# A new order of tasks, engine choices and PSUM banks in a fused scan-and-MLP kernel on one core

## The chip, the cores and the metric

The kernel runs on one core of a Trainium2 chip. The core has five engines with instruction streams of their own: TensorE (PE, matrix multiplies; PEld is its weight load), VectorE (DVE), ScalarE (ACT), GpSimd (POOL) and SyncE (SP), which here only starts DMA transfers. The metric is the device time of one execution in microseconds (us); lower is better.

## The reference, cut to what matters

All tensors are bf16; L = 2048 rows, D = 448, F = 1792.

```python
x  = A_x                                   # (1, 2048, 448)
xn = layernorm(x)
# s: a complex diagonal recurrence over the 2048 rows
Lam_bar = exp(dt * Lam);  B_bar = ((Lam_bar - 1) / Lam)[:, None] * B
Bu  = xn @ B_bar.T                         # complex, 448 states
h_t = Lam_bar * h_{t-1} + Bu_t
s   = 2 * real(h @ C.T) + xn * Dskip
# g: an MLP on a second layernorm of the same rows
y = layernorm(xn)
g = silu(gelu(y @ w1 + b1) @ w2 + b2)
out = x + s * g
```

## The kernel before

**Groups.** The 2048 rows are worked in four groups of 512 (g = 0 to 3). A group has four tiles of 128 rows, named by block b and half r. `x_all` holds x, `xn_sb` and `xn2_sb` the first and second norm, `xnT` and `xn2T` their transposes (two buffers each, used by g mod 2).

**What a group does.** VectorE takes the statistics (`ln_stats`, L430 and L434), VectorE or GpSimd turns them into scale and shift (`ln_scale`, L477 to L487), VectorE (L497) or ScalarE (L498) applies them (`ln_apply`), and a DMA transposes the result (`xt`, L507; the queue's rows show it as L106). TensorE then computes
- `mm1(g, j)`, j = 0 to 6: `xn2T` times w1 into two PSUM banks (L648), 14 matmuls of 64 rows that run in pairs; ScalarE takes them out with gelu into `gT` (L729; in group 0 some are done in halves, L741);
- `bu(g, i)`, i = 0 to 3: `xnT` times B (`BT`, and for i = 3 its copy `BT3`; L648 and L668), taken out into `u_sb` by ScalarE (L665, L670) or VectorE (L666, L671);
- `mm2(g, b)`: `gT` times w2 (L762, after a bias matmul L754), taken out by ScalarE with silu into `g_sb` (L766);
- `ym(g, b, r)`: h times C plus xn times Dskip (L780, L783), multiplied with `g_sb` by VectorE (L786); x is added (L799, L790) and the rows go out by DMA.

The recurrence itself is `ssm(g)`, on VectorE: u is turned by the table `WT` (L684 to L688), seven scans run over 512 columns each (L692), ScalarE casts the result to `s_b` (L696; L697 or, on VectorE, L698), VectorE turns it back (L712 to L716) into `h_sb`. GpSimd carries the end state to the next group (L705 to L708). The tables `WT` and the matrices `CQ` (from C) and `DG` (from Dskip, L584 on GpSimd or L585 on VectorE) are made once, in `tables`, `cq` and `parameters`.

**What sets the order.** The program records some 500 tasks; each names the tiles that it reads and writes. Three lists at the top of the file then decide everything else. `ORDER` is the one sequence in which all tasks are handed to their engines, so it is the order of every engine's stream and of the DMA queue. `SECOND` names the tasks that take the second of two engines. `BANKS` gives each PSUM tile its bank; a tile waits until the earlier tile of its bank has been read. Each engine works its stream strictly in order and waits on semaphores for what it reads:

```python
        for k in SECOND:
            (plain[k] if isinstance(k, int) else self.named[k]).choose(1)
        order = [plain[k] if isinstance(k, int) else self.named[k] for k in ORDER]
        ...
        self.place(order)
        ...
        for t in order:
            ...
            for sem, val in need.items():
                if seen.get(sem, 0) < val:
                    eng.wait_ge(self.sems[sem], val)
                    seen[sem] = val
```

**The place of the first `bu`.** `bu(0, 3)` (L668) is the first multiply by B. It needs both `xnT` transposes of group 0 and `BT3`, which VectorE copies out of `BT` (L626) and partly clears (L627); the other `bu` need all four transposed parts of B (two of the real, two of the imaginary half). All of these come through SP's one queue, between the loads of w2 and those of C, together with the broadcast of Dskip to 128 partitions (`Dbc`), the load of x for group 3 (`x_all`) and the transposes of the next group (`xn2T`).

Of the kernel before, what the change touches and what calls it, by code (L numbers as in the profile page):

```python
# [203 lines left out]


ORDER = [int(k) if k.isdigit() else k for k in """
18 17 16 4 11 12 13 14 2 3 ST I0 I4 0 10 1 I1 I2 I6 74 75 76 19 20 79 80 81 77 84 82 85 7 15 89 90 T0 78 I5 86 21 T2 I3 87 9 91 94 92 83 I7
H000 PV T1 39 6 41 8 40 88 T3 42 93 117 38 22 23 H010 95 44 H020 99 H011 103 96 H021 100 101 24 25 26 35 37 224 222 226 34 144 228 31 H04 32
104 102 105 223 118 5 54 55 H05 109 45 43 33 123 47 106 122 H001 227 115 225 229 46 111 48 110 112 124 314 49 230 97 H06 98 H03 113 193 107
56 121 125 198 DH 28 202 30 50 53 52 63 116 60 126 127 129 114 108 131 128 132 134 58 59 61 64 65 120 199 200 119 27 203 318 312 316 234 235  # L210
206 204 207 311 315 241 237 205 231 57 62 67 69 130 232 36 313 317 29 70 194 208 195 209 196 135 238 136 145 166 197 236 137 233 U00 167 66
68 U02 160 U01 164 319 324 402 400 404 401 133 162 142 161 201 141 H13 H15 320 165 323 239 163 171 240 282 H11 H14 286 283 139 168 138 287
403 170 407 284 285 406 278 H12 172 169 H10 140 279 242 H16 146 72 325 276 178 180 173 U12 147 405 177 408 148 321 288 277 247 176 149 U11
280 289 143 248 174 179 150 322 175 U10 281 181 245 H20 152 151 153 243 246 183 184 244 182 156 154 290 365 295 293 410 294 297 249 188 189
73 155 190 413 186 326 296 185 291 157 191 158 330 250 366 329 159 192 71 210 218 254 253 255 211 327 51 187 258 219 216 212 412 217 H25 298
H22 261 263 375 292 H23 260 220 369 371 376 409 372 370 252 331 251 328 U20 338 262 332 259 221 U22 333 H26 H24 377 213 256 257 339 373 265
411 214 414 378 U21 341 416 336 337 264 H35 334 H36 266 267 268 462 464 374 H31 269 335 271 272 270 H21 273 274 275 465 418 342 454 455 343
344 419 367 299 305 307 420 301 463 368 300 348 352 H32 340 H30 306 415 456 349 H34 452 457 453 347 345 H33 460 461 417 458 U31 U32 351 308
346 423 350 302 309 459 424 U30 425 354 353 379 421 426 358 355 356 422 310 357 359 382 360 427 361 362 363 364 432 431 433 440 437 428 441
429 436 383 384 466 385 388 380 394 439 438 381 215 303 443 471 386 467 387 472 396 473 430 434 435 442 447 444 445 446 469 448 449 450 390  # L220
451 395 477 475 304 389 391 392 393 397 398 481 485 489 470 474 478 399 468 476 479 480 482 483 484 486 487 488 490 I9 I8 491 492
""".split()]
SECOND = [int(k) if k.isdigit() else k for k in """
70 72 78 83 88 115 116 146 152 163 183 187 231 234 235 240 241 270 319 323 324 326 327 329 330 339 359 415 416 418 419 424
""".split()]
BANKS = [int(k) if k.isdigit() else k for k in """
4 4 4 3 4 1 2 5 2 0 1 2 4 0 4 6 6 2 0 4 6 2 2 4 0 4 0 2 0 6 7 4 5 6 1 0 5 2 4 0 3 4 0 6 6 2 4 2 4 5 6 7 4 3 5 2 2 0 4 0 0 0 6 4 2 2 6 7 6 0
1 4 2 0 7 2 6 4 5 6 2 0 0 4 6 4 3 6 2 5 0 1 7 2 4
""".split()]


# [650 lines left out]
```

## Time and profile before

| what | value |
|---|---|
| median of 3 runs | 147.53 us (147.47 to 148.44) |
| the profiled execution | 148.12 us |
| its span, first to last instruction | 146.1 us, so 2.0 us lie around it |
| busy in the span | PE 141.0, DVE 128.3, ACT 103.6, POOL 42.5 us |
| granted TensorE clock | 1.00 |

A row of the timeline gives the start in us from the span's beginning, the time from there to the end of its last instruction, engine, line, operation, output and input, a count, and in brackets the idle time ahead of it with what ended it. Neighbouring instructions of an engine overlap a little, so the distance of two starts is what one costs the engine. In the chain of work the second number is the share of the path, without overlap. Rows of the queue with SPq give the time from issue to issue; a separate view gives the time from issue to landing.

### The profile page before, as it was taken

The page shows a single profiled execution, that of the slowest core. Times are in us where ns is not written, and L with a number is a line of the kernel's source. Part 1 is how long each engine was busy: PE and PEld are TensorE (multiplying, and loading weights), DVE is VectorE, ACT ScalarE, POOL GpSimd, SP SyncE. Part 2 cuts the span into 40 slices and gives each one's busy share as a digit, 9 for nine tenths or more (in the row PEclk, how much of TensorE's full clock was granted, in tenths as well). Part 3 has the DMA queues.
Part 4 walks back from the last instruction along what each step waited for, and adds up shares of the span by engine and source line. Part 5 has one row for each costly group of instructions (what it writes and reads, how often), then busy time and mean ns, then how long its engine had stood idle before and what let it go on. Part 6 is the DMA issues. An engine that isn't in the chain of part 4 may idle for free.

```text
span 146.1 us, 2863 instructions
## 1 busy us (share of the span) xinstructions
PE 141.0 (97%) x1092; PEld 72.7 (50%) x1092; DVE 128.3 (88%) x182; ACT 103.6 (71%) x148; POOL 42.5 (29%) x88
## 2 busy tenths in 40 slices
PE   6899999979999999999999999999999999999993
PEld 1477645524554435545553454554445455555563
DVE  2942994867899999989999998999999999999994
ACT  3349999959799989999989999916996510190300
POOL 2589498710000799650000006000009400000000
PEclk9999999999999999999999999999999999999999
DMA  4999989899796300000445400044003300003033
GB/s 104 268 318 361 327 176 132 70 279 151 138 108 139 72 4 17 19 0 18 82 80 139 90 18 25 0 81 80 4 0 99 99 0 7 0 0 99 0 126 126
DMA packets 32083, 14.08 MB, mean 96 GB/s; under 512 B 24131, under 2 KB 31686, under 8 KB 32070
## 3 DMA queue, kind: packets, MB, share of 16 engines
q1 hardware_dynamic: 31376, 13.83, 43.2%
q8 instruction: 8, 0.13, 0.4%
q10 hardware_dynamic: 694, 0.07, 0.4%
q14 instruction: 5, 0.04, 0.1%
HBM read 5.63 MB, written 1.84 MB: 51 GB/s over the span
## 4 chain that ended last, share of the span: by engine, by line
PE 91%; DVE 5%; DMA 1%; issue 1%; POOL 0%; DVEq 0%
PE psum L648 42%; PE psum L762 29%; PE psum L780 14%; PE psum L668 3%; PE psum L783 2%; DVE lnst L446 2%; DMA x_all<-in_A_x_dram 1%; DVE t L786 1%; PE psum L754 1%; DVE xn_sb L451 1%; DVE tmp L790 1%; DVE lnmv L447 0%; POOL lnw L450 0%; DVE lnw L448 0%; PE psum L455 0%
## 5 line engine op out<-in xcount | busy, mean ns | idle before, releaser
L648 PE MATMUL psum<-xn2T,w_sb 64*128 64x512 bf16 (+1 forms) x434 | 44.7, 356 | 0.1
L762 PE MATMUL psum<-w_sb,gT 128*128 128x448 bf16 x224 | 43.7, 353 | 0.0
L729 ACT ACTIVATE gT<-psum,b1f 128x512 bf16<-128x512 f32 x50 | 30.8, 696 | 5.6 <-PE psum L648 5.6
L648 PEld LDWEIGHTS psum<-xn2T,w_sb 64*128 64x128 bf16 x434 | 23.5, 108 | 19.0 <-issue 1.1
L762 PEld LDWEIGHTS psum<-w_sb,gT 128*128 128x128 bf16 x224 | 21.7, 98 | 21.3 <-issue 1.3
L692 DVE TENSOR_TENSOR_SCAN s_f<-cw,cur,v_sb 128x512 f32<-128x512 f32 x21 | 25.8, 1268 | 0.1
L780 PE MATMUL psum<-CQ,h_sb 128*128 128x448 bf16 (+2 forms) x119 | 24.9, 342 | 0.0
L648 PE MATMUL psum<-xnT,BT 64*128 64x512 bf16 x168 | 20.1, 376 | 0.0
L705 POOL TENSOR_TENSOR cwk<-s_f,ang 128x8 f32<-128x8 f32 x3 | 4.3, 1425 | 43.9 <-ACT s_f L702 43.9
L498 ACT ACTIVATE xn_sb<-x_all,lnw 128x512 bf16<-128x512 bf16 x21 | 16.7, 814 | 0.1
L696 ACT ACTIVATE s_b<-s_f 128x3072 bf16<-128x3072 f32 x4 | 11.1, 2764 | 7.2 <-DVE s_f L692 7.2
L780 PEld LDWEIGHTS psum<-CQ,h_sb 128*128 128x128 bf16 x119 | 10.9, 98 | 7.4 <-issue 0.4
L766 ACT ACTIVATE g_sb<-psum 128x448 bf16<-128x448 f32 x16 | 8.2, 538 | 8.8 <-PE psum L762 8.7
L648 PEld LDWEIGHTS psum<-xnT,BT 64*128 64x128 bf16 x168 | 8.1, 94 | 10.2 <-issue 1.3
L665 ACT ACTIVATE u_sb<-psum 128x1024 bf16<-128x1024 f32 x10 | 10.3, 1027 | 0.6 <-PE psum L648 0.5
L430 DVE BATCH_NORM_STATS2 lnst<-x_all 128x6 f32<-128x448 bf16 x12 | 7.1, 607 | 3.2 <-DMA x_all<-in_A_x_dram 3.2
L786 DVE TENSOR_TENSOR t<-psum,g_sb 128x448 bf16<-128x448 f32 (+2 forms) x17 | 9.6, 583 | 0.1
L692 DVE TENSOR_TENSOR_SCAN s_f<-cw,v_sb 128x512 f32<-128x512 f32 x7 | 8.1, 1204 | 0.0
L477 POOL TENSOR_SCALAR lnw<-lnmv 128x4 f32<-128x4 f32 x2 | 1.3, 674 | 20.1 <-DVE lnmv L434 20.1
L714 DVE TENSOR_TENSOR h_sb<-pa,pb 128x3072 bf16<-128x3072 bf16 x4 | 7.0, 1755 | 0.1
L685 DVE TENSOR_TENSOR pb<-u_sb,WT 128x3072 bf16<-128x3072 bf16 x4 | 7.0, 1753 | 0.1
L684 DVE TENSOR_TENSOR pa<-u_sb,WT 128x3072 bf16<-128x3072 bf16 x4 | 7.0, 1750 | 0.1
(118 smaller groups left out, 163.5 us busy)
## 6 DMA issues: line engine op xcount, KB each, us to landing
out_dram<-tmp SPq DMA_DIRECT2D x7, 224.0 KB, 2.3
w_sb<-in_B_w_dram SPq DMA_DIRECT2D x6, 256.0 KB, 4.8
x_all<-in_A_x_dram SPq DMA_DIRECT2D x3, 448.0 KB, 6.9
w_sb<-in_B_w_dram SPq DMA_DIRECT2D x3, 448.0 KB, 9.4
u_sb<-u_sb SPq DMA_DIRECT2D x8, 64.0 KB, 1.9
s_b<-s_b SPq DMA_DIRECT2D x8, 64.0 KB, 1.9
w_sb<-in_B_w_dram SPq DMA_DIRECT2D x2, 128.0 KB, 3.5
x_all<-in_A_x_dram SPq DMA_DIRECT2D x2, 112.0 KB, 2.1
```

Source lines behind the costliest of these rows:

```text
L430: dve([lambda e, b=b, r=r, q=q: e.bn_stats(lnst[:, q, :], x_all[:, xa(2 * g + b, r), :])], [f"x{2 * g + b}"], [f"st{q}"], 0.61)
L498: ("act", lambda e: e.activation(dst, src, ACT.Identity, bias=nb, scale=rs), 0.81)]
L648: return lambda e: e.matmul(out(k), wt(k, d, halves[h]), rhs(k, d, halves[h]), start=first and d == 0, stop=not first and d == 3)
L665: kb.either(("act", lambda e: e.activation(u_sb[:, i, :, :], psum[:, bank.b:bank.b + 2, :], ACT.Copy), 1.02), ("dve", lambda e: e.tensor_c ...
L684: dve(lambda e: e.tensor_tensor(pa[:], wide(u_sb, 0), WT[:, 0:3, 1:3, :], ALU.mult), U + WK, ["pa"], 1.76)
L692: dve(lambda e, i=i, ri=ri, init=init: e.tensor_tensor_scan(s_f[:, i, ri, :], col(R1, i).to_broadcast([128, NK]), v_sb[:, i, ri, :], init, ...
L696: act(lambda e: e.activation(s_b[:, 0:3, :, :], s_f[:, 0:3, :, :], ACT.Copy), SF, ["sb"], 2.76)
L729: act([lambda e, k=k: e.activation(gT[:, gb, 2 * j + k, :], psum[:, bank.b + k, :], ACT.Gelu_apprx_tanh, bias=b1f[:, 2 * j + k:2 * j + k + ...
L762: fns = [lambda e, fi=fi, bk=bk, q=q: e.matmul(psum[:, bk.b, 0:D], gT[:, gb, fi, q * 128:(q + 1) * 128], w2_sb[:, fi, :], start=False, sto ...
L766: act(lambda e, gs=gs, bk=bk: e.activation(g_sb[:, gs, :], psum[:, bk.b, 0:D], ACT.Silu), [bk.key] + (["silu"] if g == 0 else []), [f"g{gs ...
L780: fns = [lambda e, k=k: e.matmul(psum[:, bank.b, c0:c1], h_sb[:, hb, k, k0:k0 + 128], CQ[:, k, c0:c1], start=(k == 0), stop=(k == 6)) for ...
L786: dve(lambda e: e.tensor_tensor(t3[:, ob, r, c0:c1], psum[:, bank.b, c0:c1], g_sb[:, gs, c0:c1], ALU.mult), [bank.key, f"g{gs}"], [f"t3{ob ...
```

## The change

The three lists are replaced; nothing else in the file differs. All tasks, their instructions and their sizes are the same. The start of the work (the loads of the first rows, their norm and the first transposes) keeps nearly its order; from there on the order of all engines is new.

```diff
 ORDER = [int(k) if k.isdigit() else k for k in """
-18 17 16 4 11 12 13 14 2 3 ST I0 I4 0 10 1 I1 I2 I6 74 75 76 19 20 79 80 81 77 84 82 85 7 15 89 90 T0 78 I5 86 21 T2 I3 87 9 91 94 92 83 I7
+2 3 6 11 12 13 10 8 ST 14 0 18 I2 1 17 I0 5 15 22 I6 74 16 4 I1 19 20 75 76 79 80 81 77 I4 84 82 85 T0 I7 86 78 T2 89 90 I5 I3 83 H000 87 T1
...
 SECOND = [int(k) if k.isdigit() else k for k in """
-70 72 78 83 88 115 116 146 152 163 183 187 231 234 235 240 241 270 319 323 324 326 327 329 330 339 359 415 416 418 419 424
+72 78 83 88 93 116 125 150 154 161 187 230 231 235 237 241 270 320 323 326 327 329 330 359 415 416 418 419 428 444
```

By engine: VectorE loses the subtraction over the angle table (L593), which becomes an ACTIVATE of ScalarE (L594), one copy of a transpose (L457, to ScalarE as L458), one of two wide `u_sb` casts (L666, to L665) and one small product (L585, to GpSimd). Of the 28 places where a norm is applied, VectorE had 7 and has 9 (L497), ScalarE had 21 and has 19 (L498). VectorE keeps one `ln_scale`, that of group 1 where it had that of group 2, which GpSimd now has. ScalarE loads an activation table 6 times where it did 8 times.

Three places, row for row. The first is SP's queue behind the loads of w2, before the change:

```order
L106 DMA_TRANSPOSE BT<-in_A_B_re_dram 128x2x448
L106 DMA_TRANSPOSE BT<-in_A_B_im_dram 128x2x448
L106 DMA_TRANSPOSE xnT<-xn_sb 128x8x128 x2
L106 DMA_TRANSPOSE BT<-in_A_B_re_dram 128x2x448
L107 DMA Dbc<-in_A_Dskip_dram 128x448
L106 DMA_TRANSPOSE BT<-in_A_B_im_dram 128x2x448
L107 DMA x_all<-in_A_x_dram 128x4x448
L106 DMA_TRANSPOSE xn2T<-xn2_sb 128x8x128
L107 DMA h_sb<-in_A_C_re_dram 112x4x64
L106 DMA_TRANSPOSE xn2T<-xn2_sb 128x8x128
```

The same place after the change:

```order
L106 DMA_TRANSPOSE BT<-in_A_B_re_dram 128x2x448
L106 DMA_TRANSPOSE xnT<-xn_sb 128x8x128
L106 DMA_TRANSPOSE BT<-in_A_B_im_dram 128x2x448
L106 DMA_TRANSPOSE BT<-in_A_B_re_dram 128x2x448
L106 DMA_TRANSPOSE BT<-in_A_B_im_dram 128x2x448
L106 DMA_TRANSPOSE xnT<-xn_sb 128x8x128
L107 DMA Dbc<-in_A_Dskip_dram 128x448
L106 DMA_TRANSPOSE xn2T<-xn2_sb 128x8x128
L107 DMA x_all<-in_A_x_dram 128x4x448
L106 DMA_TRANSPOSE xn2T<-xn2_sb 128x8x128
```

`Dbc` has moved from ahead of the last part of B to behind all six transposes that the first `bu` needs, and the load of `x_all` (blocks 6 and 7, group 3) has moved behind one more transpose.

The second is VectorE around the first cast of a `bu` (L666), which ends a use of two PSUM banks. Before, the statistics of group 3 (L430, L434, they read blocks 6 and 7) stand in part ahead of it and in part behind it:

```order
L497 TENSOR_SCALAR xn2_sb<-x_all,lnw 128x512
L430 BN_STATS lnst<-x_all 128x6 x2
L434 BN_AGGR lnmv<-lnst 128x2
L430 BN_STATS lnst<-x_all 128x6
L497 TENSOR_SCALAR xn2_sb<-x_all,lnw 128x512
L666 CAST u_sb<-psum 128x1024
L685 TENSOR_TENSOR pb<-u_sb,WT 128x3072
L430 BN_STATS lnst<-x_all 128x6
```

After the change, from the copy of `BT3` on:

```order
L626 COPY BT3<-BT 128x512
L627 MEMSET BT3 64x64
L434 BN_AGGR lnmv<-lnst 128x2
L497 TENSOR_SCALAR xn_sb<-x_all,lnw 128x512
L430 BN_STATS lnst<-x_all 128x6
L434 BN_AGGR lnmv<-lnst 128x2
L604 TENSOR_SCALAR WT<-WT 128x4x512
L430 BN_STATS lnst<-x_all 128x6 x3
L666 CAST u_sb<-psum 128x1024
L434 BN_AGGR lnmv<-lnst 128x2
L497 TENSOR_SCALAR xn2_sb<-x_all,lnw 128x512 x2
L684 TENSOR_TENSOR pa<-u_sb,WT 128x3072
```

All four statistics of group 3 now stand ahead of the cast, the first of them right behind the copy of `BT3`; the cast is that of `bu(0, 0)` where it was that of `bu(0, 1)`, and two norms of group 2 follow it.

The third is ScalarE in the first gelus, before and then after:

```order
L458 ACTIVATE xn2T<-psum 128x4x128
L527 ACTIVATE b1f<-b1b 128x14
L741 ACTIVATE gT<-psum,b1f 128x2x128 x10
L498 ACTIVATE xn_sb<-x_all,lnw 128x512
L729 ACTIVATE gT<-psum,b1f 128x512 x4
L553 ACTIVATE ang<-ang 128x16
L741 ACTIVATE gT<-psum,b1f 128x2x128 x2
L498 ACTIVATE xn_sb<-x_all,lnw 128x512
L729 ACTIVATE gT<-psum,b1f 128x512 x4
```

```order
L458 ACTIVATE xn2T<-psum 128x4x128
L498 ACTIVATE xn_sb<-x_all,lnw 128x512
L741 ACTIVATE gT<-psum,b1f 128x2x128 x8
L729 ACTIVATE gT<-psum,b1f 128x512 x2
L741 ACTIVATE gT<-psum,b1f 128x2x128 x2
L729 ACTIVATE gT<-psum,b1f 128x512 x2
L741 ACTIVATE gT<-psum,b1f 128x2x128 x2
L553 ACTIVATE ang<-ang 128x16
L594 ACTIVATE s_f<-s_f 128x4x512
L729 ACTIVATE gT<-psum,b1f 128x512 x4
```

A norm of group 0 now stands ahead of the first gelu, and the subtraction over the angle table ahead of the last four. In TensorE's stream the work of group 0 up to its first `bu` is the same set; behind it all of `mm1` of group 1 but one, and four of group 2, now come before the `bu` of group 1.

More of the change, by code (lines that the diff above doesn't have):

```diff
@@ L206 @@
 ORDER = [int(k) if k.isdigit() else k for k in """
-18 17 16 4 11 12 13 14 2 3 ST I0 I4 0 10 1 I1 I2 I6 74 75 76 19 20 79 80 81 77 84 82 85 7 15 89 90 T0 78 I5 86 21 T2 I3 87 9 91 94 92 83 I7
-H000 PV T1 39 6 41 8 40 88 T3 42 93 117 38 22 23 H010 95 44 H020 99 H011 103 96 H021 100 101 24 25 26 35 37 224 222 226 34 144 228 31 H04 32
-104 102 105 223 118 5 54 55 H05 109 45 43 33 123 47 106 122 H001 227 115 225 229 46 111 48 110 112 124 314 49 230 97 H06 98 H03 113 193 107
-56 121 125 198 DH 28 202 30 50 53 52 63 116 60 126 127 129 114 108 131 128 132 134 58 59 61 64 65 120 199 200 119 27 203 318 312 316 234 235
@@ L211 @@
[L211 to L218, printed above, removed]
@@ L219 @@
-346 423 350 302 309 459 424 U30 425 354 353 379 421 426 358 355 356 422 310 357 359 382 360 427 361 362 363 364 432 431 433 440 437 428 441
-429 436 383 384 466 385 388 380 394 439 438 381 215 303 443 471 386 467 387 472 396 473 430 434 435 442 447 444 445 446 469 448 449 450 390
-451 395 477 475 304 389 391 392 393 397 398 481 485 489 470 474 478 399 468 476 479 480 482 483 484 486 487 488 490 I9 I8 491 492
+2 3 6 11 12 13 10 8 ST 14 0 18 I2 1 17 I0 5 15 22 I6 74 16 4 I1 19 20 75 76 79 80 81 77 I4 84 82 85 T0 I7 86 78 T2 89 90 I5 I3 83 H000 87 T1
@@ new lines @@
+91 92 94 115 88 PV T3 38 39 55 21 23 93 54 41 H010 H020 95 117 24 56 DH 26 25 37 116 225 223 H001 96 40 31 224 103 99 33 144 100 42 43 124
+44 47 9 45 97 98 121 H04 35 48 32 34 28 H011 109 H06 104 229 227 110 101 57 122 H021 113 H05 118 105 123 312 102 114 119 106 222 228 226 49
+46 50 53 60 63 125 52 H03 111 107 193 108 198 112 230 311 58 59 313 235 7 61 64 62 65 315 202 131 316 127 126 129 317 232 231 128 237 30 27
+29 194 132 120 36 238 314 234 135 136 206 203 195 204 233 207 130 208 209 318 240 145 402 406 134 403 236 142 141 196 199 200 166 133 197
@@ new lines @@
+201 400 139 66 319 67 69 401 241 U01 U02 U00 137 205 164 160 167 165 161 404 162 H15 163 H16 68 323 H12 286 321 324 320 287 280 H10 281 288
+140 170 322 70 71 325 171 H14 276 284 172 138 51 289 H23 242 H24 405 180 277 168 177 407 175 285 148 H11 146 176 147 371 178 373 278 372 169
+173 408 179 73 279 H21 150 374 H25 367 368 375 151 149 376 174 154 155 239 U10 U11 U12 181 182 H13 247 248 245 246 282 189 243 244 H26 143
+188 190 283 H22 377 369 409 183 254 158 186 187 152 290 295 153 72 156 159 370 410 378 293 249 327 296 185 184 191 250 157 413 326 412 192
@@ new lines @@
+253 255 212 213 262 259 263 216 329 261 210 218 330 297 260 258 219 251 252 217 220 256 211 298 328 291 331 257 214 U22 U20 265 336 292 332
+411 337 414 H20 264 U21 294 266 365 333 272 268 267 334 H35 215 366 H34 335 462 H32 H31 463 269 456 457 418 338 271 273 274 275 343 342 344
+270 221 299 300 339 305 307 306 348 416 415 419 420 301 341 H36 308 302 347 454 455 350 464 H30 465 417 460 461 H33 452 340 453 458 U30 U32
+427 459 U31 352 351 421 303 349 354 309 345 346 428 353 425 423 430 422 379 355 384 380 386 426 424 310 304 429 356 360 466 382 361 362 358
@@ L222 @@
+357 363 359 364 432 431 433 473 467 381 385 439 440 437 438 436 441 443 387 434 435 442 444 446 448 447 449 396 471 390 469 468 383 445 470
+388 394 450 397 451 391 389 392 477 395 475 478 398 393 476 479 474 472 399 481 485 480 489 482 483 484 I9 I8 486 487 488 490 491 492
 """.split()]
 SECOND = [int(k) if k.isdigit() else k for k in """
-70 72 78 83 88 115 116 146 152 163 183 187 231 234 235 240 241 270 319 323 324 326 327 329 330 339 359 415 416 418 419 424
+72 78 83 88 93 116 125 150 154 161 187 230 231 235 237 241 270 320 323 326 327 329 330 359 415 416 418 419 428 444
@@ L225 @@
 """.split()]
 BANKS = [int(k) if k.isdigit() else k for k in """
-4 4 4 3 4 1 2 5 2 0 1 2 4 0 4 6 6 2 0 4 6 2 2 4 0 4 0 2 0 6 7 4 5 6 1 0 5 2 4 0 3 4 0 6 6 2 4 2 4 5 6 7 4 3 5 2 2 0 4 0 0 0 6 4 2 2 6 7 6 0
-1 4 2 0 7 2 6 4 5 6 2 0 0 4 6 4 3 6 2 5 0 1 7 2 4
+0 4 0 4 2 7 0 5 4 5 3 3 0 4 2 0 2 6 6 4 4 6 0 0 2 4 0 6 3 4 5 2 3 6 3 7 4 4 2 6 2 2 2 0 0 6 6 4 1 0 4 5 3 3 6 2 2 4 4 2 6 6 2 0 4 0 6 0 1 2
+3 1 2 4 0 0 4 6 2 2 4 6 4 0 2 6 5 4 6 7 1 5 7 6 1
 """.split()]
```

## The prediction, as it was put on record

> **What bounds the kernel now.** I read the chain of work that ended last first (its shares by engine, then its pieces in order of time), then the rows around its one gap.
>
> ```profile
> PE 91%; DVE 5%; DMA 1%; issue 1%; POOL 0%; DVEq 0%
> 9.13 9.67 PE psum L648 x126
> ...
> 19.87 10.70 PE psum L762 x56
> 30.57 0.84 issue
> 31.41 1.02 PE psum L668 x4
> 32.43 20.61 PE psum L648 x190
> ...
> 62.15 0.86 PE psum L668 x4
> ...
> 141.80 0.02 issue
> ```
>
> TensorE has work from 9.13 us to 141.80 us and stands still once, 0.84 us at 30.57, ahead of the first `bu`. Its other stretches run evenly: 56 matmuls of L762 in 10.70 us are 191 ns each, 190 of L648 in 20.61 us are 217 ns a pair. The set of matmuls is unchanged, so a new order gains only what TensorE now waits: 0.84 us, plus 0.16 us because the first L668 group takes 1.02 us and the later one 0.86. What lies ahead of 9.13 (loads, norm) and behind 141.80 (the last multiplies and stores, 4.3 us to the end of the span) keeps its order. The most there is to gain is **1.0 us**, with some tenths more for what the rows may hide.
>
> **What ended that gap.** VectorE's rows and the queue's:
>
> ```profile
> 30.63 0.30 DVE L626 COPY BT<-BT 128x512 bf16<-128x512 bf16 x1 [0.78 <-DMA BT<-in_A_B_im_dram]
> 31.19 0.11 DVE L627 MEMSET BT<- 64x64 uint32 x1
> 11.27 3.17 SPq L106 DMA_TRANSPOSE BT<-in_A_B_re_dram  x1
> 22.02 1.39 SPq L106 DMA_TRANSPOSE BT<-in_A_B_re_dram  x1
> 23.46 1.49 SPq L107 DMA_DIRECT2D Dbc<-in_A_Dskip_dram  x1
> 25.00 1.21 SPq L106 DMA_TRANSPOSE BT<-in_A_B_im_dram  x1
> 26.26 0.58 SPq L107 DMA_DIRECT2D x_all<-in_A_x_dram  x1
> 26.89 2.89 SPq L106 DMA_TRANSPOSE xn2T<-xn_sb  x1
> BT<-in_A_B_re_dram SPq DMA_TRANSPOSE x1, 9.6
> BT<-in_A_B_re_dram SPq DMA_TRANSPOSE x1, 5.0
> Dbc<-in_A_Dskip_dram SPq DMA_DIRECT2D x1, 112.0 KB, 6.1
> BT<-in_A_B_im_dram SPq DMA_TRANSPOSE x1, 5.6
> x_all<-in_A_x_dram SPq DMA_DIRECT2D x1, 448.0 KB, 5.6
> xn2T<-xn_sb SPq DMA_TRANSPOSE x1, 6.0
> ```
>
> The last six rows are times from issue to landing, in the order of the six issues above them. Added up: the first B part lands at 20.9 us, the third at 27.0, `Dbc` at 29.6, the last B part at 30.6, `x_all` at 31.9, `xn2T` at 32.9. They land in queue order, a few us behind the issue, so the queue is full and each transfer pays for those ahead. VectorE copies `BT3` at 30.63, clears it at 31.19, with a norm in between, and L668 starts at 31.41.
>
> **Part 1, the queue.** The same transfers stand ahead of the first B part (the w2 loads and b2's broadcast change places, with the same bytes in all), so it should again land near 20.9. Of what follows, only `Dbc` leaves the set that the first `bu` needs. From the third B part to `Dbc` 2.6 us pass (27.0 to 29.6), so the last of the six transposes lands near 30.6 - 2.6 = 28.0, if `Dbc` costs this; at the least it costs nothing (30.6 again), and 1.0 us, the step from `Dbc` to the last B part, would be 29.6. I take 2.6, the step that it shows itself. TensorE arrives at 30.57: it no longer waits. `BT3` needs only the B parts and no norm now stands inside it. **Gain 1.00 us.**
>
> **Part 2, x for group 3.** `x_all` of blocks 6 and 7 now has one transfer more ahead. Its price is not in the trace at this place; the nearest rows give 1.0 us (31.9 to 32.9, an `xn2T`) and at worst the 2.6 of `Dbc`; at best it is hidden. So it lands between 31.9 and 34.5; I take 32.9. This matters because VectorE now meets the first statistic of group 3 right behind `BT3`, some 4 us early, and stands there with everything behind it:
>
> ```profile
> 25.56 0.16 DVE L434 BATCH_NORM_AGGREGATE lnmv<-lnst 128x2 f32<-128x6 f32 x1
> 25.65 0.59 DVE L430 BATCH_NORM_STATS2 lnst<-x_all 128x6 f32<-128x448 bf16 x1
> 33.57 1.15 DVE L430 BATCH_NORM_STATS2 lnst<-x_all 128x6 f32<-128x448 bf16 x2
> 24.94 0.70 DVE L604 TENSOR_SCALAR WT<-WT 128x2048 bf16<-128x2048 bf16 x1 [1.98 <-ACT WT L602]
> 37.11 1.22 DVE L666 CAST u_sb<-psum 128x1024 bf16<-128x1024 f32 x1 [1.35 <-PE psum L648]
> xn2T<-xn_sb SPq DMA_TRANSPOSE x1, 4.5
> ```
>
> Behind the landing come, each from its start to the next one's, L430 (0.55), L434 (0.1), L604 (0.62), three L430 (1.65) and the cast L666 (1.22): 4.1 us with gaps 4.2, so it ends at 37.1. Its banks 4 and 5 are wanted by the second `mm1` of group 1. TensorE comes there at 30.57 + 0.86 (L668) + 4.48 (the 42 L648 of `bu`, 32.43 to 36.91 before) + 0.86 (eight matmuls of the first `mm1`) = 36.8. **Loss 0.35 us**, from 0 (landing up to 32.5) to 1.9 (at 34.5). The two norms of group 2 behind the cast end 0.7 us later, near 37.9; the two transposes behind them are issued 1.2 us apart and take 4.5 us to land (the last row, of one issued at 42.41), so the second is there near 43.6. TensorE wants it five `mm1` after 35.9, each seven pairs of 217 ns, so at 43.5 and the 0.35 lost: covered, with 0.2 us to spare.
>
> The Trainium skill, page "DMA: Bandwidth & Descriptors", section "Latency and other measured facts", gives DMA transposes an effective 261 GB/s; as an estimate by it, the seven transfers between the first B part's landing and `x_all`'s (1.79 MB, five of them transposes) take 6.8 us and one more transpose 1.0. By that, `x_all` would land near 29, the loss would be nothing and the time that of the first rival below. The trace disagrees: 11.0 us for the same seven (20.9 to 31.9).
>
> **Part 3, ScalarE in the first stage.**
>
> ```profile
> 9.85 0.24 POOL L464 TENSOR_SCALAR lnw<-lnw 128x4 f32<-128x4 f32 x1
> 10.12 3.07 ACT L741 ACTIVATE gT<-psum,b1f 128x256 bf16<-128x256 f32 x8 [0.84 <-PE psum L648]
> 18.88 2.45 ACT L729 ACTIVATE gT<-psum,b1f 128x512 bf16<-128x512 f32 x4
> 28.05 1.90 ACT L598 ACTIVATE s_f<-s_f 128x2048 f32<-128x2048 f32 x1
> ```
>
> A norm now waits ahead of the first gelu for the scale that GpSimd ends at 10.09; the gelus start near 10.87 instead of 10.12. The fourth `mm1` piece wants the first one's bank at 11.65 and gets it at 11.7: **loss 0.1 us**, bounds 0 and 0.75. L594 is not in the trace; L598 has its size and kinds, 1.80 from start to start. The last gelu of group 0 so ends near 21.9 (21.33 before); `mm2` reads it from 24.4 on, so 2.5 us cover it. Behind it stand three norms (0.7 each), a table load (1.28) and two passes over the tables (1.8 each), to 28.9; then the silu whose bank L668 wants, to 29.4, one more pass and two silus, to 32.2, whose banks the third wide `bu` wants. They are wanted at 30.57 and 33.1: 0.9 us of cover.
>
> **Part 4, VectorE, GpSimd and the end.**
>
> ```profile
> 48.27 1.02 POOL L477 TENSOR_SCALAR lnw<-lnmv 128x4 f32<-128x4 f32 x1 [18.27 <-DVE lnmv L434]
> 55.10 1.58 POOL L584 TENSOR_TENSOR DG<-ident,Dbc 128x128 bf16<-128x128 bf16 x2
> L786 DVE TENSOR_TENSOR t<-psum,g_sb 128x448 bf16<-128x448 f32 (+2 forms) x17 | 9.6, 583 | 0.1
> 56.88 1.75 DVE L712 TENSOR_TENSOR pa<-s_b,WT 128x3072 bf16<-128x3072 bf16 x1
> 136.14 0.42 DVE L716 TENSOR_TENSOR h_sb<-pa 128x512 bf16<-128x512 bf16 x1
> 137.25 0.36 PE L783 MATMUL psum<-DG,xnT 128*128 128x128 bf16 x4
> ```
>
> VectorE reaches the last h at 136.56, half a us ahead of the multiplies that read it (137.06, one matmul ahead of the quoted row). It is the second bound. Between the first L712 and there its stream loses a wide cast (1.2 us, L666 above) and takes on one L786 (0.58) and one small cast ahead of the last h: about even. It starts L712's stage near 55.9, a us earlier: ScalarE's cast of the scans (2.76) now stands behind ten gelus, which TensorE feeds until 35.9 + 10 x 1.52 + 0.35 = 51.5, so it runs from 53.1 to 55.9. So VectorE keeps its lead, 0.5 to 1.0 us, and costs TensorE nothing there. GpSimd's scale for group 2 has from about 28 us until 36.9; from 48.27 to 55.10, beside a busy VectorE, the same took 6.8 us, so it is covered too. Two table loads fewer on ScalarE save nothing on the path.
>
> **Sum.** 148.12 - 1.00 + 0.35 + 0.10 = 147.57 us, 0.55 below the profiled execution. That execution lies 0.59 above the median of its three runs, so the forecast for a median is 147.53 - 0.55 = **147.0 us**.
>
> **Rivals.**
> - *Nothing is given back*: `x_all` lands by 32.5 and ScalarE's late start is hidden. Then 1.0 to 1.2 us are gained, **146.5 us**. For it: an x load from an emptier queue could be quicker than 5.6. Against it: one transfer more ahead. Chance 0.20.
> - *The change doesn't do what it says*: the second xn transpose lands no sooner than the last B part did, or the half-us covers of parts 3 and 4 are used up, one after another, along 110 us in which two engines are full. Each costs some tenths; with the 1.0 us lost again and the 0.35 to 0.45 of losses it is **147.9 us**. For it: VectorE busy 128.3 of 146.1 us. Against it: 2.5 us of slack at the queue. Chance 0.20.
> - *Slower, the wait at `x_all`*: from a landing at 32.5 on, every us later holds VectorE's cast, and TensorE at its bank, for one us. At 35.0 the loss is 2.5 and the kernel 1% slower. A load of the same size at 7.83 took 9.3 us to land, in the fullest stretch:
>
> ```profile
> 7.83 0.72 SPq L107 DMA_DIRECT2D x_all<-in_A_x_dram  x1
> x_all<-in_A_x_dram SPq DMA_DIRECT2D x1, 448.0 KB, 9.3
> ```
>
>   Issued near 27.5, it would land at 36.8: a loss of 4.3, 150.9 us. Halfway, at 35.4, it is 2.9 and **149.5 us**. Against it: the two landings around it step by 1.0 to 1.3 us only. Chance 0.15.
>
> **How the numbers follow.** The forecast holds 0.45. Its own range is 146.7 to 147.5. With the rivals the range is 146.1 to 149.5: it leaves out the lowest part of the first (0.05) and the upper half of the last (0.08). A measurement of this kernel tells little under 1%, 1.5 us. Faster by that needs more than TensorE waits now: 0.05. Slower by that: 0.15 for the last rival and 0.02 for an unseen stall. Within 1%: 0.78.
>
> **What would show it.** Right: no idle time ahead of the first L668, which starts near 30.6; VectorE idle for 4 to 5 us on `x_all` from about 28; a short wait of TensorE near 36.8; gelus from 10.9; TensorE's last multiply near 141.3. Wrong: L668 again past 31; `x_all` past 34; any TensorE wait over 1 us; or VectorE's last L716 ending behind TensorE's arrival there.

## The result, and the profile after

The kernel after takes **148.45 us** (median of 22 executions, 148.19 to 149.51), the kernel before 147.60 (22 executions, 147.13 to 149.07): a ratio of 1.0051, 95% interval 1.0029 to 1.0073, so 0.75 us slower. The forecast was 147.0 us, 0.5 us faster; the measured time lies inside the range that was given and on the other side of the kernel before. The profiled execution of after has a span of 146.5 us. Disturbed executions are left out of all ratios and spans below, though not of the medians.

The chain of work that ended last, of the kernel after (start, us, what):

```profile
9.34 10.34 PE psum L648 x132
...
20.10 10.75 PE psum L762 x56
30.85 0.86 PE psum L668 x4
31.72 7.99 PE psum L648 x72
...
39.74 0.34 issue
40.08 1.28 ACT L729
41.38 1.27 ACT gT L729 x2
42.78 18.97 PE psum L648 x174
...
90.77 0.97 PE psum L668 x4
...
141.04 1.15 PE psum L780 x6
```

The gap ahead of the first L668 is gone, as foretold: 20.10 + 10.75 = 30.85, and L668 takes 0.86 us. Nine us later, at 39.74, there is a new piece that the chain of before did not have. It leaves TensorE and goes over ScalarE, through a table load and a gelu, and TensorE's next row starts at 42.78. The timeline of the same execution shows who waits (the bracket is the idle time ahead of the row and what ended it):

```profile
10.91 1.35 ACT L741 ACTIVATE gT<-psum,b1f 128x256 bf16<-128x256 f32 x3
26.65 0.29 DVE L626 COPY BT<-BT 128x512 bf16<-128x512 bf16 x1 [1.44 <-issue]
27.60 0.41 DVE L497 TENSOR_SCALAR xn_sb<-x_all,lnw 128x512 bf16<-128x512 bf16 x1 [0.43 <-DMA xnT<-xn_sb]
31.00 0.63 DVE L430 BATCH_NORM_STATS2 lnst<-x_all 128x6 f32<-128x448 bf16 x1 [2.99 <-DMA x_all<-in_A_x_dram]
35.75 1.22 DVE L666 CAST u_sb<-psum 128x1024 bf16<-128x1024 f32 x1 [1.73 <-PE psum L648]
36.19 5.66 PE L648 MATMUL psum<-xn2T,w_sb 64*128 64x512 bf16 x50
37.32 1.51 ACT L498 ACTIVATE xn_sb<-x_all,lnw 128x512 bf16<-128x512 bf16 x2
38.27 2.65 SPq L106 DMA_TRANSPOSE xn2T<-xn_sb  x2
40.08 1.28 ACT L729 ACT_TABLE_LOAD   x1 [1.25 <-PE psum L648]
41.38 5.31 ACT L729 ACTIVATE gT<-psum,b1f 128x512 bf16<-128x512 f32 x9
42.78 9.91 PE L648 MATMUL psum<-xn2T,w_sb 64*128 64x512 bf16 x90 [0.94 <-ACT gT L729]
57.18 1.76 DVE L713 TENSOR_TENSOR pb<-s_b,WT 128x3072 bf16<-128x3072 bf16 x1 [0.70 <-ACT s_b L696]
136.57 0.42 DVE L716 TENSOR_TENSOR h_sb<-pa 128x512 bf16<-128x512 bf16 x1
```

TensorE stands **0.94 us** until 42.78, for the bank that group 1's first gelu holds. That gelu needs the gelu table, which the silus of group 0 had displaced. ScalarE is done with its norms at 38.83 and idles 1.25 us; the load does not run in that time but starts at 40.08, once the gelu's matmuls are complete, and the gelu follows behind it. So, by the chain, 0.34 us of "issue", 1.28 of load, 1.27 of gelu and 0.14 of "issue" stand in series behind the last of these matmuls, 3.0 us in all. In the order of after, 20 other matmuls (2.17 us, at 108 ns each) run in that time before TensorE wants that pair of banks again; the rest, 0.9 us, is the stall. In the order of before there were 34 (3.7 us), and the same load in series cost nothing. Its rows, in the timeline of before:

```profile
39.53 1.28 ACT L729 ACT_TABLE_LOAD   x1 [0.80 <-PE psum L648]
40.82 4.74 ACT L729 ACTIVATE gT<-psum,b1f 128x512 bf16<-128x512 f32 x8
```

### The profile page after: what moved, and what is told of

Same layout as the page of the kernel before. It is cut to its first block, busy times and chain, and to the rows that moved or that the text cites. A ratio compares the mean times of both kernels' runs of the same rounds, so it can differ in the third digit from the quotient of the medians.

```text
span 146.5 us, 2864 instructions
## 1 busy us (share of the span) xinstructions
PE 141.7 (97%) x1092; PEld 77.2 (53%) x1092; DVE 126.2 (86%) x180; ACT 102.3 (70%) x147; POOL 37.6 (26%) x89
## 4 chain that ended last, share of the span: by engine, by line
PE 94%; ACT 2%; DVE 2%; issue 1%; DVEq 0%; ACTq 0%
PE psum L648 41%; PE psum L762 29%; PE psum L780 14%; PE psum L809 4%; PE psum L668 3%; PE psum L783 2%; PE psum L455 1%; ACT L729 1%; ACT gT L729 1%; DVE t L786 1%; PE psum L754 1%; DVE tmp L790 1%; PE psum L523 0%; DVE still L339 0%; PE psum L525 0%
## 5 line engine op out<-in xcount | busy, mean ns | idle before, releaser
L648 PEld LDWEIGHTS psum<-xn2T,w_sb 64*128 64x128 bf16 x434 | 26.5, 108 | 17.5 <-issue 1.5
L705 POOL TENSOR_TENSOR cwk<-s_f,ang 128x8 f32<-128x8 f32 x3 | 3.0, 1002 | 53.4 <-ACT s_f L702 53.4
L498 ACT ACTIVATE xn_sb<-x_all,lnw 128x512 bf16<-128x512 bf16 x19 | 14.6, 813 | 0.2 <-issue 0.2
L648 PEld LDWEIGHTS psum<-xnT,BT 64*128 64x128 bf16 x168 | 8.6, 94 | 9.7 <-issue 1.4
L665 ACT ACTIVATE u_sb<-psum 128x1024 bf16<-128x1024 f32 x11 | 10.9, 1028 | 1.1 <-PE psum L648 1.1
L430 DVE BATCH_NORM_STATS2 lnst<-x_all 128x6 f32<-128x448 bf16 x12 | 6.9, 614 | 4.8 <-DMA x_all<-in_A_x_dram 4.8
L809 PE MATMUL psum<-still 128*128 128x128 bf16 (+1 forms) x30 | 6.6, 372 | 1.2 <-DVE still L339 1.0
L713 DVE TENSOR_TENSOR pb<-s_b,WT 128x3072 bf16<-128x3072 bf16 x4 | 7.0, 1749 | 0.7 <-ACT s_b L696 0.7
L686 DVE TENSOR_TENSOR v_sb<-pa,pb 128x3072 bf16<-128x3072 bf16 x4 | 7.0, 1758 | 0.1
```

Of the source, the lines that this page charges most:

```text
L498: ("act", lambda e: e.activation(dst, src, ACT.Identity, bias=nb, scale=rs), 0.81)]
L648: return lambda e: e.matmul(out(k), wt(k, d, halves[h]), rhs(k, d, halves[h]), start=first and d == 0, stop=not first and d == 3)
L665: kb.either(("act", lambda e: e.activation(u_sb[:, i, :, :], psum[:, bank.b:bank.b + 2, :], ACT.Copy), 1.02), ("dve", lambda e: e.tensor_c ...
L686: dve(lambda e: e.tensor_tensor(v_sb[:, 0:3, :, :], pa[:], pb[:], ALU.add), ["pa", "pb"], ["v"], 1.76)
L809: pe([lambda e, idle=idle, c=c: e.matmul(psum[:, idle.b, 0:c * 128], still[:, :], still[:, None, :].to_broadcast([128, c, 128]), start=Tru ...
```

## The experiments

Theory T: the loss is the table load in series with the gelu behind one wait, with too few matmuls to cover it. Rival N: ScalarE is late because two norms stand ahead of that gelu. Rival E: the time is lost in many small places. Times are medians; each kernel was compared with executions of the kernel before on the same chip, and the ratio is to those. It is not the ratio of the two medians, so a difference by it can be some tenths of a us from that of the medians.

In the lists, Hgj stands for the first eight matmuls of `mm1(g, j)`: H15 opens group 1's first `mm1` in after, 286 is its last six matmuls, 287 its gelu. H14 is the next user of its pair of banks. 321 and 324 are the two norms on ScalarE ahead of that gelu, and LG is an added load of the gelu table.

**The first mm1 whole earlier**

```diff
-404 162 H15 163 H16 68 323 H12 286 321 324 320 287
+404 162 H15 286 163 H16 68 323 H12 321 324 320 287
```

> The kernel after, with the last six matmuls of group 1's first mm1 (task 286) put directly behind its first eight, so that its pair of banks is whole some 2.3 us earlier. Theory T (the load of the gelu table waits for the same matmuls as the gelu behind it, so that 1.28 + 1.27 us stand between the last matmul and the free bank, and only 20 matmuls, 2.17 us, cover them): the load now starts when the two norms on ScalarE end, at 38.8, the bank is free at 41.4, and TensorE wants it at 41.85: the stall of 0.94 is gone, time 148.45 - 0.94 = 147.5 us, 0.1 below the kernel before. Theory N (the two norms that ScalarE took over make it late): they still end at 38.8 and the stall stays at 0.7 to 0.94, time 148.2 to 148.45. Theory E (the time was lost elsewhere, in many places): stall gone, but less than 0.5 us of it is seen in the time.

148.11 us, ratio 1.0024 (0.9993 to 1.0055). Timeline of this kernel:

```profile
38.80 1.28 ACT L729 ACT_TABLE_LOAD   x1
44.96 7.75 PE L648 MATMUL psum<-xn2T,w_sb 64*128 64x512 bf16 x70 [0.56 <-DMA xn2T<-xn_sb]
```

The load starts as T said, directly behind the norms, and the stall near 42 is gone. Only 0.3 to 0.4 of the expected 0.9 us arrive. In the profiled execution TensorE reaches group 2's first `mm1` before its second transpose has landed (44.82) and waits 0.56 us there; in the kernel after, the stall had covered this. That execution has the longest span of its twelve (146.6 us, the others 145.9 to 146.4), so what the median one lost there is not known. By the time alone, less than 0.5 us, this run falls to theory E; the next one decides.

**The table loaded ahead, nothing moved**

```diff
+            kb.tag = "LG"
+            preload("gelu_apprx_tanh_and_others", [], "gelu1", "gelu")
```
```diff
-321 324 320 287 280 H10
+321 324 320 LG 287 280 H10
```

> The kernel after, with an explicit load of the gelu table on ScalarE ahead of group 1's first gelu, that waits for nothing; no other instruction is moved. T: the load runs from 38.8, right behind the norms, to 40.1, the gelu starts at 40.1 as soon as its matmuls are done, its bank is free at 41.4, TensorE's stall of 0.94 at 41.85 is gone: 147.5 us. N: ScalarE gets no time back, the stall stays: 148.2 to 148.45 us. E: stall gone, less than 0.5 us seen in the time.

147.56 us, ratio 0.9984 (0.9954 to 1.0014): against the 1.0051 of after 0.67% or 1.0 us less. Timeline:

```profile
38.61 1.28 ACT L348 ACT_TABLE_LOAD   x1
39.91 5.89 ACT L729 ACTIVATE gT<-psum,b1f 128x512 bf16<-128x512 f32 x10
```

The same load without a wait runs in ScalarE's idle time, the gelu starts 1.47 us earlier than in after (0.23 of it because `mm2` began at 19.87 in this execution and at 20.10 in that one), and TensorE's waits hold nothing near 42. That is T, and it leaves rival E little: one added instruction gives back more than the whole loss against the kernel before.

**The two norms on VectorE.** `SECOND` gets 321 and 324.

> The kernel after, with the two norms that stand on ScalarE ahead of group 1's first gelu (tasks 321 and 324, 0.75 us each) given to VectorE. T: ScalarE then idles longer ahead of the table load, which still starts with the last matmul of the first mm1 at 40.1; the stall of 0.94 stays, time 148.45 us, plus or minus 0.2. N: ScalarE is 1.5 us earlier, the stall is gone, 147.5 us.

148.24 us, ratio 1.0024 (0.9983 to 1.0065). Timeline:

```profile
39.66 1.28 ACT L729 ACT_TABLE_LOAD   x1 [2.35 <-PE psum L648]
42.36 9.90 PE L648 MATMUL psum<-xn2T,w_sb 64*128 64x512 bf16 x90 [0.63 <-ACT gT L729]
```

ScalarE now idles 2.35 us and the load still waits for the matmuls; a stall of 0.63 us stays. N is out as the whole cause. It is not without a part: the stall is 0.3 us shorter, where T had it unchanged. In the chain of after 0.34 us of "issue" stand between the last matmul and the load (39.74), and here only 0.03; why, no run tells.

**The kernel before with less cover.** H12, the next user of those banks, now comes behind H11 and H14 (16 matmuls) instead of behind 34.

```diff
-282 H11 H14 286 283 139 168 138 287 403 170 407 284 285 406 278 H12 172
+282 H11 H14 283 H12 286 139 168 138 287 403 170 407 284 285 406 278 172
```

> The kernel before with less cover behind group 1's first mm1: the first half of the next mm1 that takes its pair of banks (H12) is moved from 34 matmuls behind it to 14 (behind H11 and H14, which makes 16 with the two halves of 8). T: the bank is free 1.28 + 1.27 + 0.14 = 2.7 us behind the last matmul, 16 matmuls of 108 ns cover 1.73, so TensorE stalls 0.95 us near 40 and the time is 147.6 + 0.95 = 148.55 us. If the load is not in series with the gelu, 1.4 us are needed, the cover is enough and the time stays 147.6 us.

149.67 us, ratio 1.0106 (1.0060 to 1.0152). Timeline:

```profile
39.01 1.28 ACT L729 ACT_TABLE_LOAD   x1 [0.81 <-PE psum L648]
41.71 4.10 PE L648 MATMUL psum<-xn2T,w_sb 64*128 64x512 bf16 x34 [1.06 <-ACT gT L729]
46.02 1.71 PE L648 MATMUL psum<-xn2T,w_sb 64*128 64x512 bf16 x14 [0.20 <-ACT gT L729]
```

The first stall is 1.06 us where 0.95 was worked out, in the kernel that never showed it: the cover decides. The whole cost was undersized, 1.6 us by the ratio. Task 286, here the last six matmuls of the `mm1` whose gelu comes next, now stands behind H12, and TensorE waits for ScalarE once more at 46. The two waits add up to 1.26 us; the other 0.3 the trace does not show.

**What the gap of before was worth: two more profiles of it, unchanged.**

> The kernel before, unchanged: one more profiled execution. The spans of 35 executions of it lie between 145.0 and 147.7 us, those of the kernel after between 146.3 and 146.6. Theory V (the gap ahead of the first L668 differs between executions, since the last B part lands in a full queue, and the profiled execution with 0.84 us of it was one of the later ones): the span is 145.1 plus the gap ahead of L668, so with a span of 145.0 to 145.4 there is no gap or one under 0.3. Theory W (the pace of TensorE's first matmuls makes the difference): the gap is again 0.8 whatever the span, and the span moves with the start of the first long run of L648 (9.13 in the first profile).

> The kernel before, unchanged, once more, with the same expectations: by V the span is 145.1 plus the gap ahead of the first L668; by W the gap is 0.8 whatever the span.

147.87 and 148.00 us, spans 145.8 and 146.0. The chain of the first of them:

```profile
30.82 0.41 issue
31.22 1.02 PE psum L668 x4
```

The gap is 0.41 us here and 0.43 in the second, half of the 0.84 on which the forecast was built. V holds for the gap. Its formula for the span does not: 145.1 + 0.41 is 0.3 short, since TensorE's first long run also started 0.25 us later (9.38 against 9.13).

**The queue's part alone, on the kernel before**

```diff
-69 130 232 36 313 317 29 70 194
+69 130 232 313 317 29 36 194
-196 135 238 136 145 166
+196 135 136 70 238 145 166
```

> The kernel before with one part of the change alone: D's broadcast (task 36) behind the last B part in the queue, and on VectorE the clearing of BT3 directly behind its copy and the first product with D behind both. V: the last B part lands a step earlier, at 29.6 or sooner, and the gap ahead of the first L668 is gone in nearly all executions; where there was none, nothing is gained: spans 145.0 to 145.2 throughout instead of 145.0 to 147.7, median 147.15 us, 0.4 to 0.5 below the kernel before. W: the gap of 0.84 was there in every execution, so all get 0.8 to 1.0 faster: spans from 144.0, median 146.6 to 146.8 us. If the order in the queue does not matter: 147.6 us and the same spread.

**147.09 us**, ratio 0.9954 (0.9926 to 0.9981), the fastest of all. Its chain, and the copy of `BT3` in its timeline:

```profile
19.88 10.70 PE psum L762 x56
30.58 0.86 PE psum L668 x4
31.44 20.61 PE psum L648 x190
```
```profile
23.82 1.86 SPq L106 DMA_TRANSPOSE BT<-in_A_B_im_dram  x1
29.27 0.29 DVE L626 COPY BT<-BT 128x512 bf16<-128x512 bf16 x1
```
```profile
BT<-in_A_B_im_dram SPq DMA_TRANSPOSE x1, 4.2
```

By the last row (issue to landing) the last part of B lands at 28.0, and the copy waits for nothing. The edit also puts the clearing of `BT3` right behind its copy, ahead of a norm, as after does. The copy ends at 29.56, a us ahead of TensorE's arrival at 30.58, so in this execution the norm between them (0.41 us) would not have held TensorE: the gain is the queue's. The spans of its executions lie between 145.0 and 145.3 us; those of the kernel before, beside it, between 145.0 and 147.0. So the change of the queue does what it says, and takes away a spread of up to 2 us that some executions have and others do not: 0.5 us between the medians, 0.7 by the ratio, not 1.0.

**The head**

```diff
-ST 14 0 18 I2 1 17 I0 5 15 22 I6 74 16 4 I1 19 20 75 76 79 80 81 77 I4 84 82 85 T0
+ST 14 0 18 I2 1 17 I0 5 15 22 74 16 4 I1 19 20 75 76 79 80 81 77 I4 I6 84 82 85 T0
```

> The kernel after, with the four 128-wide warm-up matmuls (I6) that stand among the 512-wide ones moved behind these, as in the kernel before. Theory W (the order of the warm-ups sets how soon TensorE runs at full pace: four 128-wide transposes at 5.45 take 0.58 us after and 0.38 before): they take 0.38 again, the first long run of L648 starts near 9.1 instead of 9.3, time 148.45 - 0.2 = 148.25 us. Rival: the slow transposes come from how the first loads land, or from chance between executions: 0.58 again, no change, 148.45.

148.31 us, ratio 1.0038 (1.0007 to 1.0069). The first transposes in this kernel, and then in the one with the table loaded ahead, whose head is that of after:

```profile
5.23 0.61 PE L455 MATMUL psum<-ident,xn_sb 128*128 128x128 bf16 x4
```
```profile
5.29 0.38 PE L455 MATMUL psum<-ident,xn_sb 128*128 128x128 bf16 x4
```

The order of the warm-up matmuls is not the cause. One order gives 0.58 and 0.38 in two kernels, and the kernel before gave 0.38 in its first profile and 0.61 in the next. The time differs between executions of one order, and from what, no run shows; so the 0.21 us by which after's first long run starts later than before's in the two profiles can't be put down to the change.

**What is left without the stall.** First the bias matmuls of `mm2` earlier:

```diff
-H03 111 107 193 108 198
+H03 111 193 107 108 198
```

> The kernel after with the table load ahead, and besides it the four bias matmuls (task 193) that open group 0's mm2 moved six matmuls earlier, ahead of the last half of mm1, where the kernel before has them. Theory: the 0.12 to 0.14 us that TensorE stands between them and the first mm2 matmul is the drain behind the matmul that writes the same bank, hidden if six others stand between; 0.15 to 0.2 us less than with the table load ahead alone: 147.4 us, span 145.3. Rival: the pause moves with them, no change, 147.56.

147.81 us, ratio 1.0010 (0.9979 to 1.0041): no gain, a miss. The waits of TensorE (what for, total us, times, longest), in this kernel and in the one with the table load alone:

```profile
PE psum L648 <- DMA xn2T<-xn_sb: 0.3, 1, 0.3
```
```profile
PE psum L762 <- PE psum L754: 0.2, 1, 0.2
```

The pause behind the bias is gone from the trace, and TensorE waits for group 2's second transpose again. From the queue to its landing this took 4.77 us in the profile of this kernel, and 4.39 in that of the one with the table load alone, where it landed 0.04 us ahead of TensorE:

```profile
39.44 4.77 DMA xn2T<-xn_sb
```
```profile
39.44 4.39 DMA xn2T<-xn_sb
```

So there is no room left at this place, and the landing, which no edit here touched, decides. This profile too is of the longest span of its kernel (146.2 us of 145.5 to 146.2). Then all named losses at once; beside the two edits, the norms ahead of the cast:

```diff
-167 165 161 404 162 H15 163 H16 68 323 H12 286 321 324 320 287
+167 165 320 321 323 324 161 404 162 H15 163 H16 68 H12 286 LG 287
```

`SECOND` gets 321 and 324.

> The kernel after with every loss that was named taken away at once: the gelu table loaded ahead, the bias matmuls of group 0's mm2 six matmuls earlier, and the four norms of group 2 that feed the transposes of xn2 all on VectorE in its idle 1.7 us ahead of the wide cast L666 (two of them stood on ScalarE, all behind casts of u), so that the two transposes are issued near 35.5 instead of 38.0 and land near 41. Theory: the wait of TensorE for these transposes (0.56 in the run with the whole first mm1, 0.26 in the run with the earlier bias, none in one other) is gone in every execution; TensorE then runs without a stop from L668 to its last multiply, spans 145.0 to 145.5 us, median 147.2 us, as in the kernel before with the queue change alone. Rival: other small waits remain, and the spans stay between 145.5 and 146.2 us, median 147.6.

148.28 us, ratio 1.0033 (0.9995 to 1.0071). Timeline:

```profile
33.22 0.63 DVE L430 BATCH_NORM_STATS2 lnst<-x_all 128x6 f32<-128x448 bf16 x1 [4.54 <-DMA x_all<-in_A_x_dram]
36.15 1.37 DVE L497 TENSOR_SCALAR xn_sb<-x_all,lnw 128x512 bf16<-128x512 bf16 x4
37.43 1.22 DVE L666 CAST u_sb<-psum 128x1024 bf16<-128x1024 f32 x1
38.80 14.44 PE L648 MATMUL psum<-xn2T,w_sb 64*128 64x512 bf16 x132 [1.17 <-DVE lnmv L434]
```

Both expectations failed. `x_all` landed at 33.2 in this execution (31.0 in that of after), the four norms that I had put behind it added 1.3 us, the cast that frees the bank ran until 38.65, and TensorE stood 1.17 us (the bracket names L434, a short instruction that ends 0.1 us behind the cast). Spans go from 145.3 to 147.2 us. This is the mechanism of the prediction's part 2 and of its last rival, brought about by moving work onto the path behind a load.

**The kernel after, timed again**

> The kernel after, unchanged, on the same chip as the last one and timed again. If its stall at the table load is the same in every execution and the gap ahead of the first L668 never comes back, its spans stay within 146.3 to 146.7 us, the stall near 42 is 0.9 again and the time is 148.45 us, whether the first transposes take 0.38 or 0.58.

148.24 us, ratio 1.0050 (1.0014 to 1.0085), spans 146.3 to 146.8 us: nearly as steady as expected, without the spread of the kernel before. This run has no trace that tells the size of the stall. The run with the warm-ups moved, whose order is that of after from there on, shows it once more:

```profile
42.61 9.90 PE L648 MATMUL psum<-xn2T,w_sb 64*128 64x512 bf16 x90 [0.94 <-ACT gT L729]
```

**The account**, by ratios: the kernel before 0; with the queue's part alone -0.46%, or -0.7 us; after with the table loaded ahead -0.16%, or 0.44 us above that; after +0.51%, or 1.0 us above that again. The intervals of the first two overlap, but their spans do not (145.0 to 145.3 and 145.5 to 146.2 us), so something is left. What makes up the 0.44 us is not shown: the 0.2 us of pause behind the bias and waits for group 2's transposes of 0 to 0.56 us were seen, with `x_all` as a third where VectorE has more to do behind it.

## Why the prediction was right and wrong

- **Part 1, the queue: mechanism right, value oversized.** The last part of B was there by 26.65; the last of the six transposes, for which 28.0 was forecast, is now the second `xnT`, there by 27.60 (the norm that overwrites its source starts then). TensorE did not wait, L668 took 0.86 us. The value of 1.00 us was that of one execution. The two others that were profiled had a gap of 0.41 and 0.43, and with the queue's part alone the kernel gained 0.5 us between the medians and 0.7 by the ratio. The text noticed that the profiled execution lay 0.59 us above the median and took this for an offset that before and after share; part of it may have been the very gap that the change removes: the two later profiles, 147.87 and 148.00 us, have half of it.
- **Part 2, x for group 3: the term was too large, and of the right kind.** `x_all` landed at 31.0, below the 31.9 to 34.5 that were allowed; the cast waited 1.73 us for TensorE and not for x, and the loss was 0 instead of 0.35. That a later landing turns into a stall was shown by the run with all losses taken away. The "0.2 us to spare" for group 2's transposes were none once nothing else held TensorE: 0.56 and 0.26 us of waiting in two kernels, and 0.04 us to spare in a third.
- **Part 3, ScalarE: the step that failed.** The gelus started at 10.91 (10.87 forecast), no bank was late in the first stage. But the walk along ScalarE ended with the silus and the casts of `bu`. It priced the table load ahead of the silus and not the second one, ahead of group 1's first gelu; and part 4 said that "two table loads fewer on ScalarE save nothing on the path", without asking what stands behind those that stay. The row was there, in the trace of before: a load with 0.80 us of idle time ahead of it that ended with TensorE's matmuls. Read as it stands, it says that the load waits for the same matmuls as its gelu, so a bank comes free 2.7 us behind its last matmul, and the new order has 2.17 us of cover: a stall of 0.5 us, enough to use up the forecast gain. The 0.34 us of "issue" ahead of the load in after, which make it 0.94, this row does not show. The missing term is 0.94 us in the profile and 1.0 us by the runs, and turns the forecast's sign.
- **Part 4, VectorE and the end: right, its size apart.** L712's stage (now begun by L713) starts at 57.18, where 55.9 was forecast, with a loss of 0.35 us in it that did not come; the stall of 0.94 and the first L668 at 30.85 instead of 30.57 are most of the difference. The last L716 starts at 136.57, and no VectorE row holds TensorE at the end. The last multiply ends at 142.19 instead of 141.3.
- **The sum.** Forecast were -1.00 + 0.35 + 0.10 = -0.55 us. By the runs it is -0.7 for the queue, 0 for the two losses, +1.0 for the table load and +0.44 that no term named: +0.75.
- **The rivals.** None named the table load. The first one's condition held (x by 32.5, nothing lost to ScalarE's late start) and its 146.5 us did not come. The slower one had its place at `x_all`, which held VectorE for 2.99 us and TensorE not at all. Of "the change doesn't do what it says" the first half was wrong and the second, covers of half a us used up one after another, may be the 0.44 us that are left.
- **What was to show it wrong**, "any TensorE wait over 1 us", was missed by 0.06 us.

## What to carry to other kernels

Where an order is made anew, count for each reuse of a bank the work between its last matmul and its next, and set against it everything that its reader does in series, a table load included; a table load placed ahead, where its engine idles, cost nothing here. A wait for a queue in one profiled execution is a sample: hold the profiled time against the median and the spread before a gap is booked as gain. When a stall goes, the wait that it covered comes up, so a part of a change that helps by itself (here the queue's order on the old kernel, 147.09 us) can be worth more than the whole.

## What the runs showed of the hardware

- The load of the gelu table that is not placed by hand started only with the gelu's own operands (0.80 us of idle time ahead of it in before, 1.25 in after, 2.35 with the norms moved away); placed by hand it ran 0.01 us behind the norms. It took 1.28 us each time, and the gelu, where its matmuls were done by then, started 0.02 us behind it. The Trainium skill, page "ScalarE: Activation LUTs", section "What ACT_TABLE_LOAD costs", states about 1283 ns for the load, which the rows confirm, and 1380 ns of drain with every switch, which no row here shows behind the load.
- The pace of TensorE's first matmuls differs between executions of one program: four 128-wide transposes near 5.3 us took 0.38 or 0.58 to 0.61 us with a granted clock of 1.00 in both. The Trainium skill, page "TensorE: Matmul & The Clock Gate", section Part 1: The HAM clock gate (the "warmup" mystery), tells of a window that runs freely, so that the same kernel starts with a differing number of slow matmuls. The spread between executions fits this; that it is the cause, the rows do not show, since the granted clock is 1.00 in both.
- One load of x for group 3, behind nearly the same queue, landed 4.2 us after its issue in one execution (26.77 to 31.0) and 5.0 in another (28.22 to 33.2), issued 1.45 us later. Of the 2.2 us by which it landed later, 1.45 lie ahead of the issue and 0.8 in the transfer.
